# Clustered attention, a Fourier mix and a feed-forward layer on one core: scales of the weights from sums on TensorE, a later product with the values, and a cast moved to GpSimd

## The chip, the cores and the metric

The kernel runs on one core of a Trainium2 chip. A core has five engines that run on their own and wait for each other through semaphores: TensorE (PE, matrix products; its weight loads are shown apart as PEld), VectorE (DVE), ScalarE (ACT), GpSimd (POOL) and SyncE (SP, which here issues every DMA, in order). The metric is the device time of the whole program in microseconds (us), the median of the runs.

## The reference

Attention over 4 sequences of 768 tokens, 8 heads of 64; a query sees only the keys that are nearest to the same one of 16 centroids. Then a two-dimensional Fourier transform whose real part is added, a normalisation, and a feed-forward layer.

```python
mask = q_assign[:, :, :, None] == k_assign[:, :, None, :]
scores = np.where(mask, scale * np.matmul(q, k.transpose(0, 1, 3, 2)), -1e9)
attn = np.exp(scores - np.max(scores, axis=-1, keepdims=True))
attn = attn / (np.sum(attn, axis=-1, keepdims=True) + 1e-09)
x = np.matmul(attn, v)                       # heads side by side: (4, 768, 512)
u = x + np.real(np.fft.fft(np.fft.fft(x, axis=1), axis=2))
un = (u - mean(u)) / np.sqrt(var(u) + 1e-06)
out = u + np.maximum(un @ w_ch1, 0.0) @ w_ch2        # 512 x 2048 and 2048 x 512
```

The two weight matrices come as 64-bit floats. Products are made in 16-bit floats, with each operand split in a high and a low half.

## The kernel before, in words

`Overlap.run` lays the program out in ticks. Heads go in pairs: 4 pairs for a sequence, 16 in all. In each tick one strip of 128 queries of a pair gets its scores (`Attention.scores`), and the strip that stood `LAG` = 2 ticks earlier is multiplied with the values (`attend`). Six ticks make a pair, 24 a sequence. The next pair's preparation (`prep`: loading q and k, their scales, the split in halves, the cluster assignment, a one-hot table) is spread over the ticks before it. The order on TensorE is the order in which this code is written; on the other engines a scheduler sets it, with costs of its own, and the queues then run strictly in that order.

One strip of scores goes through all engines, twice, for the two heads of the pair (j = 0, 1). TensorE writes 128x768 scores in PSUM (L320, L325). VectorE scales them by a negative factor, writes the result (`ju`) and leaves the row's minimum in `m` (L339). ScalarE takes the exponential: in the first sequence ("early", `pr < 4`) from `ju`, which then lies in the not yet used second token buffer `X` (L343); in the later ones from the scores in PSUM (L345), and `ju` is then only a bfloat16 by-product. ScalarE casts the result to 16 bits, the high half (L353; `ph` for the first head, `p` for the second in the early ones). GpSimd subtracts to get the low half (L354). SyncE sends both through a transposing DMA to `pt` (L356), of which there are `PT` = 5, and TensorE multiplies `pt` with the values (L374 to L376) into `ps_o`, which VectorE empties after every third strip (L386 to L390).

The weights are made ready during the first sequence, by `Weights.run`, a step for each of 32 tiles of 128x512, 0.684 ticks apart. A tile's 512 KB land in one of 8 raw buffers. ScalarE turns the topmost 16 bits of each number in two patterns by sign (`signs`, L519 and L520), TensorE joins them (`join`, L528), VectorE puts in the lower bits (L532), and `halve` writes the scaled high and low halves. The scale is a power of two from the largest number: VectorE reduces every tile's top bits to its largest (`largest`, L491). For the first matrix four tiles share one scale over all partitions (L496, a broadcast `along` TensorE and L504); for the second each tile has its own for each partition, four at a time. `top_power` then makes the scale in four small instructions (L58 to L61), on 128x1 or 128x4 numbers. `relative` joins the scales of both matrices at the end.

From the second sequence on, the previous sequence's Fourier transform (`Fourier`) and feed-forward layer (`FeedForward`, L858 up and L888 down) are filled in between the ticks.

Of the kernel before, what the change touches and what calls it, by code (L numbers as in the profile page):

```python
# [16 lines left out]
I32 = mybir.dt.int32  # L17
# [36 lines left out]

def top_power(nc, tops, s, inv):

    t = tops.bitcast(I32)
    nc.vector.tensor_scalar(out=t, in0=t, scalar1=20, scalar2=None, op0=ALU.logical_shift_right)  # L58
    nc.vector.tensor_scalar(out=t, in0=t, scalar1=-910.0, scalar2=1.0, op0=ALU.add, op1=ALU.max)
    nc.vector.tensor_scalar(out=inv.bitcast(I32), in0=t, scalar1=240.0, scalar2=float(1 << 23), op0=ALU.min, op1=ALU.mult)  # L60
    nc.vector.reciprocal(out=s, in_=inv)  # L61
# [20 lines left out]
class Attention:  # L82
# [22 lines left out]
    EX = 1  # L105
    PC = ()

# [201 lines left out]
    def scores(self, pr, st):  # L309
        nc, sb = self.nc, self.sb  # L310
        assert self.ready >= pr
        (hq, hk), oh, (e, ne) = self.hl[pr], self.oht[pr], self.sc.scores(pr)
        sl = slice(st * P, (st + 1) * P)
# [13 lines left out]
        for j in range(2):  # L327

            m = sb.tile([P, 1], F32, name="rmx", tag="rmx", bufs=6)
            early = pr < H // 2  # L330
            if early:

                n = (2 * st + j) % self.RING * S
                p32 = self.X[1].rearrange("p a x -> p (a x)")[:, n:n + S]
            else:
                p32 = sb.tile([P, S], F32, name="p32", tag="p32", bufs=2)
            x = p32.rearrange("p (h x) -> p h x", h=2)
            ju = x if early else sb.tile([P, 2, SH], BF16, name="ju", tag="ju")
            self.mark = nc.vector.tensor_scalar(out=ju, in0=ps[j][:, :, 0:SH], scalar1=ne, scalar2=None, op0=ALU.mult, op1=ALU.min,  # L339
                                    accum_out=m)  # L340
            self.late = m
            if early:
                nc.scalar.activation(p32, p32, AF.Exp, bias=m, scale=-1.0)  # L343
            else:
                nc.scalar.activation(x, ps[j][:, :, 0:SH], AF.Exp, bias=m, scale=e)  # L345
            if early and j:
                ph = sb.tile([P, S], F32, name="p32", tag="p32", bufs=2).bitcast(F16).rearrange("p (a x) -> p a x", a=2)
            else:
                ph = sb.tile([P, 2, S], F16, name="ph", tag="ph", bufs=2)
            if early and j and (st in self.PC):  # L350
                nc.gpsimd.tensor_copy(out=ph[:, 0], in_=p32)
            else:
                nc.scalar.copy(out=ph[:, 0], in_=p32)  # L353
            nc.gpsimd.tensor_tensor(out=ph[:, 1], in0=p32, in1=ph[:, 0], op=ALU.subtract)  # L354
# [79 lines left out]
class Weights:  # L434
# [6 lines left out]

    RAW, PN = tuple(4128 * i for i in range(6)) + (29696, 33824), (24768, 26816)
    ID, TOP, MX = 28864, 29376, 29472
    X32 = 37952, 40000
    EXTRA, A2, AHEAD = 0, 9, 7

    def __init__(self, tc, pool, arena, psf, w1, w2, ident):
# [5 lines left out]

        self.inv = [pool.tile([P, n], F32, name=f"winv{n}") for n in (4, 16)]
        self.rel = pool.tile([P, 16], F32, name="wrel")
# [29 lines left out]

    def largest(self, k):

        nc, at = self.nc, self.arena.at
        g, i = divmod(k, 4)
        mx = at(self.MX + 32 * (g % 2), [P, 4], F32)  # L490
        nc.vector.tensor_reduce(out=mx[:, i:i + 1], in_=self.top(k).bitcast(BF16), op=ALU.max, axis=AX.X,  # L491
                                apply_absolute_value=True)
        if i == 3 and g >= 4:
            self.scales(g, mx)
        elif i == 3:
            nc.vector.tensor_reduce(out=mx[:, 0:1], in_=mx, op=ALU.max, axis=AX.X)  # L496

    def block(self, g):

        nc, at = self.nc, self.arena.at  # L500
        mx = at(self.MX + 32 * (g % 2), [P, 4], F32)
        ps = self.psf()
        along(nc, ps[:, 0:P], mx[:, 0:1], self.ident)
        nc.vector.tensor_reduce(out=mx[:, 1:2], in_=ps[:, 0:P], op=ALU.max, axis=AX.X)  # L504
        self.scales(g, mx[:, 1:2])

    def scales(self, g, mx):
        n = mx.shape[1]
        s = self.sb.tile([P, 4], F32, name="wsc", tag="wsc", bufs=2)
        top_power(self.nc, mx, s[:, 0:n], self.inv[0][:, g:g + 1] if n == 1 else self.inv[1][:, 4 * (g - 4):4 * (g - 3)])  # L510
        for i in range(4):
            self.scale[4 * g + i] = s[:, i % n:i % n + 1]

    def signs(self, k):

        nc, at = self.nc, self.arena.at
        pn = at(self.PN[k % 2], [P, 2, DM], BF16)
        top = self.top(k)
        nc.scalar.activation(pn[:, 0].bitcast(I16), top.bitcast(I16), AF.Relu, bias=self.off[:, 0:1], scale=8.0)  # L519
        nc.scalar.activation(pn[:, 1].bitcast(I16), top, AF.Relu, bias=self.off[:, 1:2], scale=8.0)  # L520
        self.bits[k] = pn

# [11 lines left out]
    def halve(self, k):  # L534
# [4 lines left out]
        if k % 2:  # L539
            x = self.arena.at(self.X32[k // 2 % 2], [P, DM], F32)  # L540
            nc.scalar.activation(x, ps, AF.Copy, scale=s)
# [4 lines left out]
    def run(self):  # L546
# [5 lines left out]
        for i in range(2):  # L552
            nc.gpsimd.tensor_scalar(out=self.idb[:, i], in0=self.ident, scalar1=1.0 - 2 * i, scalar2=None, op0=ALU.mult)
        for k in range(-self.AHEAD, 33):
            if k >= 1 and k % 4 == 1 and k < 16:
                self.block(k // 4)
# [14 lines left out]
    def relative(self):  # L571

        nc, at = self.nc, self.arena.at
        top, m1, r = (at(self.TOP + 32 * j, [P, 1], F32) for j in range(3))
        rel = self.rel
        nc.vector.tensor_tensor(out=rel.rearrange("p (a c) -> p a c", c=4),
                                in0=self.inv[1].rearrange("p (a c) -> p a c", c=4),
                                in1=self.inv[0].rearrange("p (a o) -> p a o", o=1).broadcast_to([P, 4, 4]), op=ALU.mult)
        nc.vector.tensor_reduce(out=m1, in_=rel, op=ALU.max, axis=AX.X)
        ps = self.psf()  # L580
        along(nc, ps[:, 0:P], m1, self.ident)
        nc.vector.tensor_reduce(out=top, in_=ps[:, 0:P], op=ALU.max, axis=AX.X)
        nc.vector.reciprocal(out=r, in_=top)
        nc.vector.tensor_scalar(out=rel, in0=rel, scalar1=r[:, 0:1], scalar2=HSC, op0=ALU.mult, op1=ALU.mult)
        nc.vector.tensor_scalar(out=self.dsc, in0=top, scalar1=1.0 / HSC, scalar2=None, op0=ALU.mult)

# [34 lines left out]
class Fourier:  # L621
# [25 lines left out]
    def fold(self, b):  # L647
# [4 lines left out]
        s = self.scale[b][0]  # L652
        mid = at(self.XM, [1, M + 1], F32)
        nc.gpsimd.tensor_copy(out=mid, in_=X[0:1, 3, 0:M + 1])
        nc.gpsimd.tensor_tensor(out=mid[:, 1:M], in0=mid[:, 1:M], in1=X[0:1, 3, DM - 1:M:-1], op=ALU.add)
        last = at(self.XL, [P, 3], F32)
        xt = {}
        for i, op in self.FOLDS:
# [8 lines left out]
            nc.sync.dma_start(out=t, in_=h.rearrange("p a t x -> p (a t x)"), transpose=True)  # L667
            xt[i] = t.rearrange("p (a t c) x -> p a t c x", a=2, t=3)
        self.parts[b] = xt, last, mid, s

# [117 lines left out]
USC = 200  # L788
HSC = float(2.0 ** -20)


class FeedForward:


    NT = 2 * P
    HH, HL, OSB, HR = 0, 8192, (16384, 18432), (28736, 29760)
# [48 lines left out]
    def up(self, blk):  # L845
# [6 lines left out]
        for f in range(16):  # L852
# [8 lines left out]
            r = at(self.HR[f % 2], [P, self.NT], F32)  # L861
            if f % 2:
                nc.vector.tensor_scalar(out=r, in0=ps, scalar1=rel[:, f:f + 1], scalar2=0.0, op0=ALU.mult, op1=ALU.max)  # L863
            else:
                nc.scalar.activation(r, ps, AF.Relu, scale=rel[:, f:f + 1])
            nc.scalar.activation(hh[:, f], ps, AF.Relu, scale=rel[:, f:f + 1])  # L866
            nc.gpsimd.tensor_tensor(out=hl[:, f], in0=r, in1=hh[:, f], op=ALU.subtract)  # L867
# [29 lines left out]

PT = 5


class Overlap:
# [22 lines left out]
    F2 = 1  # L924
    PIN, PF, PV = (), 29, 1
    CE, WP, WQ = 0.45, 0, 0

# [53 lines left out]
    def run(self):  # L981
# [43 lines left out]
        for pr in range(NP):  # L1025
# [36 lines left out]
def cluster_attention_fourier_ffn_kernel(ctx, tc, q, k, v, cent, w1, w2, cd, sd, cm, cs, ss, ny, out):  # L1062
# [5 lines left out]
    sc = Scales(nc, glob)  # L1068
    arena = Arena(glob, 47264)
    pf = ctx.enter_context(tc.tile_pool(name="ps_f", bufs=3, space=PSUM))  # L1070
# [46 lines left out]
```

## Time and profile before

| | |
|---|---|
| three runs | 1055.57, 1049.64, 1053.56 us; median 1053.56 |
| the profiled execution | 1049.91 us, its span 1048.1 us |
| busy in the span | PE 910.8 us (87%), DVE 627.4 (60%), ACT 625.3 (60%), POOL 586.9 (56%) |
| DMA queue of SP | 138.50 MB, 65.9% of 16 engines |
| first scores of pairs 0, 1, 2, 3 and 4 read by VectorE | at 31.1, 75.9, 125.6, 170.9 and 208.5 us |

How to read the page: the digits of its second part are tenths of a slice of 26.2 us in which an engine was busy; PEclk is the granted clock of TensorE; the DMA row is the mean busy share of the 16 DMA engines, and as a number it can go above 1, since packets overlap. A group's row tells its line, engine, operation, what it writes and reads, the count, busy time, the mean of one in ns, and the idle time of the engine before it with what ended that.

### The profile page before, as it was taken

The numbers are of one execution on the slowest core, as the hardware profiler recorded it, in microseconds if no ns is written. First come the engines' busy times: TensorE is split into PE (matmuls) and PEld (weight loads), VectorE is DVE, ScalarE is ACT, GpSimd is POOL, SyncE is SP. The second block draws the span as 40 slices with busy tenths as digits, with TensorE's granted clock in tenths as the row PEclk, the third lists the DMA queues.
The fourth block names the chain that finished last, engine by engine and source line by source line (L and its number), as shares of the span: only waits on it lengthen the run. The fifth ranks groups of instructions, "written<-read, shape, count | busy, mean of one in ns | idle before, by whom it ended". The sixth has DMA issues, their size and how long they took to land.

```text
span 1048.1 us, 23542 instructions
## 1 busy us (share of the span) xinstructions
PE 910.8 (87%) x9350; PEld 591.7 (56%) x9362; DVE 627.4 (60%) x1297; ACT 625.3 (60%) x980; POOL 586.9 (56%) x693
## 2 busy tenths in 40 slices
PE   3665565749899999998899999997999999999998
PEld 2333333425575756655666757555757667576674
DVE  8789899767757555668656555667555333631110
ACT  4798889755766665645666746556756543351230
POOL 2364565753975756655856646647847645271230
PEclk9987878769899999999899999998999999999999
DMA  7799998979887776568877767588757562321000
GB/s 272 179 225 245 196 239 166 171 156 153 177 123 153 128 154 121 121 137 161 153 137 142 140 128 132 110 141 170 124 102 133 96 110 43 81 52 31 11 11 21
DMA packets 396239, 140.01 MB, mean 134 GB/s; under 512 B 381784, under 2 KB 381792, under 8 KB 396128
## 3 DMA queue, kind: packets, MB, share of 16 engines
q1 hardware_dynamic: 396128, 138.50, 65.9%
q8 instruction: 73, 1.20, 0.5%
q14 instruction: 38, 0.31, 0.1%
HBM read 42.52 MB, written 6.29 MB: 47 GB/s over the span
## 4 chain that ended last, share of the span: by engine, by line
PE 39%; DVE 6%; DMA 3%; ACT 3%; POOL 2%; issue 2%; SPq 0%; ACTq 0%; DVEq 0%; POOLq 0%
PE ps_f L888 16%; PE ps_f L858 13%; PE ps_big L320 3%; DMA pt<-ph 3%; PE ps_f L713 2%; DVE ju L339 1%; ACT p L345 1%; PE ps_o L374 1%; POOL ph L354 1%; PE ps_o L375 1%; PE ps_o L376 1%; PE ps_big L325 1%; ACT ph L353 1%; DMA scr<-in_k_dram 0%; DVE arena L660 0%
## 5 line engine op out<-in xcount | busy, mean ns | idle before, releaser
L354 POOL TENSOR_TENSOR ph<-p,ph 128x768 f16<-128x768 f32 x144 | 242.9, 1688 | 184.6 <-ACT ph L353 150.1
L858 PE MATMUL ps_f<-arena,w1h 128*128 128x256 f16 x1536 | 271.4, 277 | 19.1 <-ACT arena L866 9.0
L888 PE MATMUL ps_f<-w2h,arena 128*128 128x512 f16 x768 | 238.9, 379 | 0.0
L345 ACT ACTIVATE p<-ps_big,rmx,sce 128x768 f32<-128x768 f32 x144 | 142.1, 988 | 132.9 <-DVE ju L339 127.5
L858 PE MATMUL ps_f<-arena,w1l 128*128 128x256 f16 x768 | 212.4, 277 | 0.0
L339 DVE TENSOR_SCALAR_CACHE_REDUCE ju<-ps_big,sce 128x768 bf16<-128x768 f32 x144 | 146.1, 1014 | 68.2 <-PE ps_big L325 58.2
L888 PEld LDWEIGHTS <-arena 128*128 128x128 f16 x1152 | 108.7, 98 | 126.6 <-issue 5.2
L858 PEld LDWEIGHTS <-w1h 128*128 128x128 f16 x1536 | 152.1, 99 | 36.0 <-issue 14.3
L867 POOL TENSOR_TENSOR arena<-arena 128x256 f16<-128x256 f32 x192 | 128.1, 677 | 77.3 <-ACT arena L866 73.6
L320 PE MATMUL ps_big<-hlk,hlq 64*128 64x384 f16 x1152 | 128.9, 348 | 39.0 <-ACT p L345 23.4
L374 PE MATMUL ps_o<-v,pt 128*128 128x66 f16 x1152 | 124.8, 198 | 43.0 <-DVE X L390 27.5
L888 PE MATMUL ps_f<-w2l,arena 128*128 128x512 f16 x384 | 145.5, 379 | 0.0
L374 PEld LDWEIGHTS <-pt 128*128 128x128 f16 x1152 | 110.2, 100 | 57.7 <-issue 37.1
L353 ACT CAST ph<-p 128x768 f16<-128x768 f32 x144 | 119.6, 832 | 15.0 <-DMA pt<-ph 12.8
L375 PE MATMUL ps_o<-v,pt 128*128 128x64 f16 x1152 | 124.8, 199 | 0.0
L376 PE MATMUL ps_o<-v,pt 128*128 128x66 f16 x1152 | 124.5, 198 | 0.0
L866 ACT ACTIVATE arena<-ps_f,wrel 128x256 f16<-128x256 f32 x192 | 90.1, 472 | 54.8 <-DVE arena L863 54.7
L863 DVE TENSOR_SCALAR arena<-ps_f,wrel 128x256 f32<-128x256 f32 x96 | 46.3, 482 | 124.9 <-PE ps_f L858 66.4
L320 PEld LDWEIGHTS <-hlq 64*128 64x128 f16 x1152 | 55.5, 99 | 101.5 <-issue 72.7
L375 PEld LDWEIGHTS <-pt 128*128 128x128 f16 x1152 | 110.7, 101 | 2.8
L376 PEld LDWEIGHTS <-pt 128*128 128x128 f16 x1152 | 111.1, 103 | 0.0
L858 PEld LDWEIGHTS <-w1l 128*128 128x128 f16 x768 | 76.1, 99 | 20.2 <-issue 10.7
(178 smaller groups left out, 1330.4 us busy)
## 6 DMA issues: line engine op xcount, KB each, us to landing
arena<-in_moe_w_ch_dram SPq DMA_DIRECT2D x32, 512.0 KB, 6.8
scr<-in_q_dram SPq DMA_DIRECT2D x16, 384.0 KB, 2.9
scr<-in_k_dram SPq DMA_DIRECT2D x16, 384.0 KB, 4.5
vst<-in_v_dram SPq DMA_DIRECT2D x16, 384.0 KB, 3.5
out_dram<-arena SPq DMA_DIRECT2D x24, 256.0 KB, 2.3
pt<-ph SPq DMA_TRANSPOSE x168, 3.9
arena<-in_cs_dram SPq DMA_DIRECT2D x12, 192.0 KB, 3.5
arena<-in_ss_dram SPq DMA_DIRECT2D x12, 192.0 KB, 3.5
```

Of the source, the lines that this page charges most:

```text
L320: nc.tensor.matmul(out=ps[j][:, hf, 0:SH], lhsT=hq[rows[j], a, sl], rhs=hk[rows[j], c, hs], start=(i == 0), stop=False)
L339: self.mark = nc.vector.tensor_scalar(out=ju, in0=ps[j][:, :, 0:SH], scalar1=ne, scalar2=None, op0=ALU.mult, op1=ALU.min, accum_out=m)
L345: nc.scalar.activation(x, ps[j][:, :, 0:SH], AF.Exp, bias=m, scale=e)
L353: nc.scalar.copy(out=ph[:, 0], in_=p32)
L354: nc.gpsimd.tensor_tensor(out=ph[:, 1], in0=p32, in1=ph[:, 0], op=ALU.subtract)
L374: nc.tensor.matmul(out=o[:, at:at + W], lhsT=hi, rhs=v16[:, kt, 0:W], start=(kt == 0), stop=False)
L375: nc.tensor.matmul(out=o[:, at:at + D], lhsT=hi, rhs=v16[:, kt, 66:130], start=False, stop=False)
L376: nc.tensor.matmul(out=o[:, at:at + W], lhsT=lo, rhs=v16[:, kt, 0:W], start=False, stop=(kt == ST - 1))
L858: nc.tensor.matmul(out=ps.rearrange("p (t x) -> p t x", x=P), lhsT=a[:, dc, fs], rhs=c[:, :, dc], start=(i == 0), stop=(i == 11))
L866: nc.scalar.activation(hh[:, f], ps, AF.Relu, scale=rel[:, f:f + 1])
L867: nc.gpsimd.tensor_tensor(out=hl[:, f], in0=r, in1=hh[:, f], op=ALU.subtract)
L888: nc.tensor.matmul(out=ps, lhsT=a[:, f, ts], rhs=c[:, f], start=(i == 0), stop=(i == 47))
```

## The change

The largest number of a tile is no longer searched. The two sign patterns of four tiles (a group) are summed over the partitions by eight products with a matrix of ones (`block`, L490), all in one PSUM tile; the largest entry of that sum, its exponent taken, gives one scale for the group, in both matrices. `signs` handles two tiles in one instruction, with three buffers for the patterns. `top_power` writes to PSUM and works on 128x1 in all eight groups. In the first sequence the high half of the second head is cast by GpSimd (L347). In later sequences `ju` is written in place in PSUM as a float, and ScalarE reads it from there. The product with the values comes three ticks behind the scores in the first 22 strips, with six `pt`. `relative` is shorter, and GpSimd's two small instructions for `mid` come after the folds.

```diff
-    PC = ()
...
-            ju = x if early else sb.tile([P, 2, SH], BF16, name="ju", tag="ju")
+            ju = x if early else ps[j][:, :, 0:SH]
...
-            if early:
-                nc.scalar.activation(p32, p32, AF.Exp, bias=m, scale=-1.0)
-            else:
-                nc.scalar.activation(x, ps[j][:, :, 0:SH], AF.Exp, bias=m, scale=e)
+            nc.scalar.activation(x, ju, AF.Exp, bias=m, scale=-1.0)
...
-            if early and j and (st in self.PC):
+            if early and j:
                 nc.gpsimd.tensor_copy(out=ph[:, 0], in_=p32)
...
-    def largest(self, k):
...
-        nc.vector.tensor_reduce(out=mx[:, i:i + 1], in_=self.top(k).bitcast(BF16), op=ALU.max, axis=AX.X,
-                                apply_absolute_value=True)
...
+        ps = self.psf()
+        i = 0
+        for k in range(4 * g, 4 * g + 4):
+            for j in range(2):
+                nc.tensor.matmul(out=ps, lhsT=self.ones[:, 0:1].broadcast_to([P, P]), rhs=self.bits[k][:, j], start=(i == 0), stop=(i == 7))
+                i += 1
+        mx = at(self.MX + 32 * (g % 2), [P, 1], F32)
+        nc.vector.tensor_reduce(out=mx, in_=ps, op=ALU.max, axis=AX.X)
+        s = self.sb.tile([P, 1], F32, name="wsc", tag="wsc", bufs=2)
+        top_power(nc, mx, ps[:, 0:1], s, self.inv[g // 4][:, g % 4:g % 4 + 1])
...
-            if 0 <= k + 3 < 32:
-                self.largest(k + 3)
-            if 0 <= k + 1 < 32:
-                self.signs(k + 1)
+            if k % 2 == 0 and 0 <= k + 2 < 32:
+                self.signs(k + 2)
+            if k % 4 == 0 and 0 <= k < 32:
+                self.block(k // 4)
...
-PT = 5
+PT = 6
...
-                at(t0 + st + self.LAG, 3, att.attend, pr, st)
+                at(t0 + st + self.LAG + (6 * pr + st < self.LATE), 3, att.attend, pr, st)
```

What the queues make of it is shown at three places. The first is VectorE's queue where the second matrix gets its first group's scale, in the third pair of heads; `arena` holds the raw weights, `X_64` the early `ju`. Before:

```order
L491 TENSOR_REDUCE arena<-arena 128x1
L544 SCALAR_TENSOR_TENSOR w2l<-ps_f,wsc,w2h 128x512
L58 TENSOR_SCALAR arena<-arena 128x4
L59 TENSOR_SCALAR arena<-arena 128x4
L60 TENSOR_SCALAR winv_86<-arena 128x4
L61 RECIPROCAL wsc<-winv_86 128x4
L491 TENSOR_REDUCE arena<-arena 128x1
L532 SCALAR_TENSOR_TENSOR ps_f<-arena,ps_f 128x512
```

After:

```order
L493 TENSOR_REDUCE arena<-ps_f 128x1
L518 SCALAR_TENSOR_TENSOR ps_f<-arena,ps_f 128x512
L58 TENSOR_SCALAR ps_f<-arena 128x1
L215 TENSOR_REDUCE amx<-scr 128x1
L59 TENSOR_SCALAR ps_f<-ps_f 128x1
L60 TENSOR_SCALAR winv_86<-ps_f 128x1
L61 RECIPROCAL wsc<-winv_86 128x1
```

The reductions L491 of single tiles are gone; one reduction of a group's sum (L493) stands ahead of the four small instructions, which are now one number wide.

The second is TensorE's queue ahead of the first scores (L320 before), where the first pair's transposes (L271 before, L270 after) end. Before:

```order
L271 MATMUL ps_f<-ident,ac 128x128 x3
L528 LDWEIGHTS arena
L528 MATMUL ps_f<-arena 128x512
L528 LDWEIGHTS arena
L528 MATMUL ps_f<-arena 128x512
L48 MATMUL ps_f<-ident,amx 128x128 x3
```

After, the end of the eight products of the first group's sum, of which the last three are shown, and the join (now L514):

```order
L490 LDWEIGHTS arena
L490 MATMUL ps_f<-arena 128x512
L490 LDWEIGHTS arena
L490 MATMUL ps_f<-arena 128x512
L490 LDWEIGHTS arena
L490 MATMUL ps_f<-arena 128x512
L514 LDWEIGHTS arena
L514 MATMUL ps_f<-arena 128x512
L514 LDWEIGHTS arena
L514 MATMUL ps_f<-arena 128x512
```

Such a run of eight products comes eight times, each time with a tick's scores queued behind it.

The third is GpSimd's queue at the first strips of the first pair. Before:

```order
L354 TENSOR_TENSOR ph<-X_64,ph 128x768
L354 TENSOR_TENSOR p_299<-X_64,p_299 128x768
L542 TENSOR_TENSOR w1l<-arena,w1h 128x512
L189 COPY vst<-rmx 128x1
L354 TENSOR_TENSOR ph<-X_64,ph 128x768
```

After:

```order
L347 CAST p_310<-X_64 128x768
L350 TENSOR_TENSOR ph<-X_64,ph 128x768
L528 TENSOR_TENSOR w1l<-arena,w1h 128x512
L350 TENSOR_TENSOR p_310<-X_64,p_310 128x768
L188 COPY vst<-rmx 128x1
L347 CAST p_357<-X_64 128x768
```

The second head's cast stands ahead of the first head's subtraction.

More of the change, by code (lines that the diff above doesn't have):

```diff
@@ L434 @@
 class Weights:
[L442 to L444 removed]
+    RAW, PN = tuple(4128 * i for i in range(6)) + (29696, 33824), (24768, 40000, 44096)
+    ID, TOP, MX, ONE = 28864, 29376, 29472, 29568
+    X32 = 37952
     EXTRA, A2, AHEAD = 0, 9, 7
@@ L452, in __init__ @@
         self.dsc = pool.tile([P, 1], F32, name="dsc")
-        self.inv = [pool.tile([P, n], F32, name=f"winv{n}") for n in (4, 16)]
+        self.inv = [pool.tile([P, 4], F32, name=f"winv{n}") for n in range(2)]
         self.rel = pool.tile([P, 16], F32, name="wrel")
```

81 lines of the change are left out of this document (33 added, 48 removed).

## The prediction

> **What bounds the kernel now.** I read the busy time by stage first, to see where time can come from at all. Columns: window, its length, busy time and count of each engine, granted TensorE clock, DMA share, GB/s.
>
> ```profile
> core 0: us, PE busy (x) PEld busy (x) DVE busy (x) ACT busy (x) POOL busy (x), PEclk, DMA share, GB/s
> 0.00:31.00 31.00, 12.95 (x52) 6.60 (x53) 25.04 (x72) 15.15 (x24) 5.54 (x38) 1.00 0.68 239
> 31.00:208.00 177.00, 110.58 (x1313) 65.58 (x1324) 151.08 (x311) 153.17 (x219) 105.02 (x90) 0.83 0.96 207
> 208.00:1048.00 840.00, 787.26 (x7987) 519.56 (x7985) 451.27 (x915) 456.95 (x739) 476.32 (x566) 0.97 0.60 114
> ```
>
> The three windows are the start, the first sequence's strips and the rest. In the rest TensorE is busy 787.3 of 840 us (94%), and none of its products there is touched. In the middle 177 us it works only 62%, while DVE (85%) and ACT (87%) are nearly full, and so are the DMA engines. By pair of heads:
>
> ```profile
> 31.00:76.00 45.00, 29.00 (x314) 15.74 (x318) 35.65 (x84) 39.76 (x58) 25.95 (x20) 0.92 0.98 215
> 76.00:125.60 49.60, 28.00 (x358) 17.25 (x358) 44.55 (x89) 43.09 (x63) 28.48 (x26) 0.83 0.95 228
> 125.60:171.00 45.40, 29.23 (x348) 17.60 (x351) 41.98 (x82) 40.71 (x59) 26.36 (x22) 0.77 0.99 209
> 171.00:208.00 37.00, 24.35 (x300) 14.99 (x300) 28.91 (x61) 29.61 (x42) 24.22 (x22) 0.77 0.88 164
> ```
>
> The fourth pair, with no L491 left and few weights, takes 37 us; the three others take 45 to 50. Then TensorE's waits from 25 to 210 us (engine, tile, line, by whom, us in total, times, longest):
>
> ```profile
> PE ps_o L374 <- DVE X L390: 27.5, 6, 5.5
> PE ps_big L320 <- DVE X L339: 14.8, 17, 3.7
> PE ps_o L374 <- DMA pt<-p: 8.6, 8, 2.6
> PE ps_o L374 <- DMA pt<-ph: 6.8, 4, 2.2
> ```
>
> It waits mostly for DVE. Last, one such wait from inside: DVE's timeline before the first scores of the third pair (start, length).
>
> ```profile
> 116.50 1.61 DVE L59 TENSOR_SCALAR arena<-arena 128x4 int32<-128x4 int32 x1
> 118.15 1.56 DVE L60 TENSOR_SCALAR winv<-arena 128x4 int32<-128x4 int32 x1
> ...
> 123.38 1.71 DVE L236 SCALAR_TENSOR_TENSOR hlq<-scr,scp,hlq 128x768 f16<-128x768 f32 x1 [0.52 <-ACT hlq L235]
> 125.01 0.67 DVE L491 TENSOR_REDUCE arena<-arena 128x1 f32<-128x512 bf16 x1
> 125.60 1.00 DVE L339 TENSOR_SCALAR_CACHE_REDUCE X<-ps_big,sce 128x768 f32<-128x768 f32 x1
> ```
>
> and POOL's at the same time:
>
> ```profile
> 116.44 1.64 POOL L354 TENSOR_TENSOR ph<-X,ph 128x768 f16<-128x768 f32 x1 [0.41 <-DVE w2l L544]
> 118.05 1.64 POOL L354 TENSOR_TENSOR p<-X,p 128x768 f16<-128x768 f32 x1
> ...
> 123.12 1.15 POOL L542 TENSOR_TENSOR w2l<-arena,w2h 128x512 f16<-128x512 f32 x1
> ```
>
> Two instructions on four numbers last 1.6 us each, and each ends within 0.03 us of a POOL subtraction's end (118.11 and 118.08; 119.71 and 119.69): they sit out POOL's instruction. So the stage is DVE's and ACT's, in strict order, with DMA close behind.
>
> **The change part by part.** The rows of the groups (whole run or the first 210 us, which for these are the same):
>
> ```profile
> L491 DVE TENSOR_REDUCE arena<-arena 128x1 f32<-128x512 bf16 x32 | 21.7, 680 | 8.0 <-DMA arena<-in_moe_w_ch_dram 7.9
> L504 DVE TENSOR_REDUCE arena<-ps_f 128x1 f32<-128x128 f32 x4 | 1.1, 284 | 0.6 <-PE ps_f L48 0.6
> L59 DVE TENSOR_SCALAR arena<-arena 128x4 int32<-128x4 int32 x4 | 4.6, 1143 | 0.1
> L60 DVE TENSOR_SCALAR winv<-arena 128x4 int32<-128x4 int32 x4 | 6.2, 1547 | 0.1
> L59 DVE TENSOR_SCALAR arena<-arena 128x1 int32<-128x1 int32 x4 | 0.6, 148 | 0.0
> L60 DVE TENSOR_SCALAR winv<-arena 128x1 int32<-128x1 int32 x4 | 0.6, 151 | 0.1
> L519 ACT ACTIVATE arena<-arena 128x512 int16<-128x512 int16 x32 | 24.1, 753 | 4.6 <-PE ps_f L528 1.6 <-PE ps_o L376 1.5 <-DMA scr<-in_q_dram 1.5
> L343 ACT ACTIVATE X<-X,rmx 128x768 f32<-128x768 f32 x48 | 44.1, 935 | 9.3 <-DVE X L339 7.6 <-POOL ph L354 1.4 <-issue 0.3
> L353 ACT CAST p<-X 128x768 f16<-128x768 f32 x24 | 20.0, 833 | 0.0
> L528 PE MATMUL ps_f<-arena 128*128 128x512 bf16 x52 | 22.0, 510 | 6.8 <-DVE w1l L544 4.6 <-DVE arena L58 1.0 <-issue 0.7
> ```
>
> DVE. Gone: 21.7 (L491), 1.1 (L504), 10.8 (the 4-wide L59 and L60). Added: eight reductions of 512 sums, 0.68 each as L491 (5.4), and four more groups of 1-wide L59 and L60 (4 x 0.30 = 1.2). L58 and L61 stay at eight each. Net 33.6 - 6.6 = 27 us less. Eight of the L491 lie before 31 us (columns as in the first windows, of L491 alone):
>
> ```profile
> 0.00:31.00 31.00, 5.41 (x8) 1.00 0.68 239
> ```
>
> so the stage loses about 22 us of DVE's 151.
>
> ACT. 24 casts go: 20.0. The 64 sign patterns of 512 become 32 of 1024. L519 and L343, both with a pointer as bias, give (935 - 753)/256 = 0.71 ns an element, so 1.12 us: 32 x 1.12 = 36 against 64 x 0.75 = 48, 12 less (ends: 0, if 1024 costs twice 512, and 15). Together 32, of which some 29 in the stage.
>
> POOL gets the 24 casts. No such cast is in the trace; the nearest copies are these, the upper end is L354, with two inputs, at 1.64:
>
> ```profile
> L882 POOL COPY arena<-X 128x512 f32<-128x512 f32 x4 | 2.5, 612 | 0.0
> L654 POOL COPY arena<-X 1x257 f32<-1x257 f32 x4 | 1.6, 391 | 0.1
> ```
>
> 221 ns for 255 elements more, so 0.83 us for 768, which I take as nearest in kind: 20 us (ends 15 and 39). POOL goes from 105 to 125 of the stage. The cast takes as long as ACT's 0.83 and runs beside ACT's cast of the first head, so both `pt` are issued no later.
>
> TensorE gets 64 products like L528: 22.0/52 = 0.42 us each, 27 us, eight at a time, 3.4 us ahead of a tick's scores. Its sign patterns are queued on ACT before the exponentials of the ticks ahead, so I see no wait for ACT there. TensorE goes from 111 to some 135: it stays below DVE and has 66 us of waits in the stage to lose.
>
> The third tick of distance gives the `pt` transposes 7 us more to land; that removes the 15.4 us of waits for `pt` above, and part of the 27.5 for `ps_o`, which is DVE's lateness; I count both as how the relief comes through, not again. With six `pt`, a transpose now waits for the product three strips back, which is queued right behind this tick's scores, while the transpose needs DVE, ACT and POOL first (L339 1.00, L343 0.94, L353 0.83 and L354 1.64, 4.4 us): no wait.
>
> `ju` in PSUM (144 times, after 208 us): a DVE write to PSUM costs 688 ns (L532) where one to SBUF costs 737 (L544), both with 512 elements:
>
> ```profile
> L532 DVE SCALAR_TENSOR_TENSOR ps_f<-arena,ps_f 128x512 uint32<-128x512 uint32 x32 | 21.5, 688 | 3.3 <-PE ps_f L528 3.2
> L544 DVE SCALAR_TENSOR_TENSOR w2l<-ps_f,wsc,w2h 128x512 f16<-128x512 f32 x8 | 5.9, 737 | 0.0
> PE ps_big L320 <- ACT p L345: 10.1, 8, 3.0
> ```
>
> ACT already waited for DVE's minimum, so the chain is the same; TensorE's products hide it. The last row is what TensorE waits there for `ps_big` after 260 us. I take 0, ends -4 and +4. The later `mid` and the shorter `relative` are 1 us each off the path: 0.
>
> DMA moves the same bytes, and is next. Its best over 25 us is here:
>
> ```profile
> 50.00:75.00 25.00, 15.48 (x193) 9.36 (x192) 20.11 (x52) 23.70 (x35) 17.02 (x13) 0.86 1.07 224
> 75.00:100.00 25.00, 14.67 (x216) 9.41 (x218) 23.18 (x46) 21.83 (x33) 12.26 (x11) 0.80 1.07 252
> ```
>
> **The sum.** The stage holds 0.96 x 177 = 170 us of DMA work; at 1.07 that needs 159 us, 18 less than now. By DVE, 129 us at its 85% make 151 us, 26 less. DMA ends first: I take 16 of its 18. In the start the eight L491 (5.4 us, on a DVE busy 81%) stand partly between the first pair's steps: 3 less (ends 0 and 5). Total -19: 1049.9 - 19 = 1031 against the profiled execution, whose span is 1048.1. That execution lies 3.7 below the median of the runs shown (1053.56); a new kernel's median may lie off its best as well, so 1032.
>
> A page would give more: by "DMA: Bandwidth & Descriptors" of the Trainium skill, section "Latency and other measured facts", a transposing DMA reaches 261 GB/s; moving the stage's 207 GB/s x 177 us at that rate is, as an estimate, 140 us, so DMA would not bind and the sum would be -29, 1021. The trace never held more than 252 GB/s there, with the share at 1.07, so I keep the bound.
>
> **The rivals.**
> (a) DMA holds the stage as it is: its share is 0.95 to 0.99 over three pairs already, and overlapping packets may be no reserve. Against it: 1.07 over 50 us, and DMA waits of 15 us beside 42 for DVE. Only the start and 2 us come: 1045 to 1050.
> (b) All of DVE's relief comes through: 26 + 5: 1018 to 1022. For it: the fourth pair's 37 us; against: DMA.
> (c) Slower: TensorE's sums come before the scores in a queue in strict order. If their 27 us lie open, they eat the relief of 19: +8, 1058. That decides from 70% of them uncovered. Against it: the 66 us TensorE idles there.
> (d) POOL's casts hold DVE. L236 at 123.38 lasted 1.71, where 768 elements take L339 1.00, beside POOL's instruction of 123.12. If each of 24 casts did that for its 0.83 us, 20 us would go: 1050. "SBUF — State Buffer" of the Trainium skill, "Who interferes with whom", has the rule: VectorE in a two-port mode, or with two SBUF inputs, and GpSimd share a port pair under an exclusive lock. The two fences of 116 to 120 us agree. But only L236, L201 and the one-hot steps, some 7 a pair, are of that kind, and the 4-wide ones leave.
>
> **How the numbers follow.** Forecast (1024 to 1041) 0.60; (b) 0.14; (a) 0.13; (d) 0.06; (c) 0.07. The range reaches from (b)'s 1018 into (a), 1047. A change below 0.5% (5.3 us) can't be told from none. Faster, below 1048.3: 0.60 + 0.14 + 0.10 of (a) = 0.84; same: the rest of (a) and (d) 0.09; slower 0.07.
>
> **What would show it.** Right: first scores of the fifth pair at DVE near 189 instead of 208.5 us; DVE busy near 600; DMA share above 1.0 from 50 to 170 us; the casts on POOL near 0.83 us; the later stretch as long as before. Wrong: a stage near 177 us with the DMA share unchanged (a); TensorE waiting at the sums, or scores late behind them (c); longer L235 and L200 rows (d); POOL over 90% in the stage, if the cast costs as much as a subtraction.

## The result, and the profile after

Slower, where the prediction said faster: 1060.57 us median (1058.07 to 1062.89, 6 runs) against 1051.39 for the kernel before on the same chip (1049.64 to 1055.57, 6 runs). The ratio is 1.0081, with a 95% interval of 1.0059 to 1.0103. The forecast was 1032, its range 1018 to 1047.

The windows of the changed kernel, cut at the same places as before (first scores of the first and the fifth pair; same columns):

```profile
29.80:215.00 185.20, 121.50 (x1324) 69.43 (x1343) 136.05 (x287) 130.28 (x165) 123.02 (x114) 0.77 0.90 199
215.00:1057.80 842.80, 790.58 (x8017) 521.87 (x8016) 449.98 (x913) 441.81 (x737) 477.66 (x566) 0.97 0.59 114
```

The first sequence takes 185.2 us instead of 177, the rest 842.8 instead of 840. VectorE's work there fell from 151 to 136 us and ACT's from 153 to 130 (some 129 and 124 were forecast), and both are used less: VectorE 73% of the stage (it was 85%), ACT 70% (87%), GpSimd 66%, DMA 0.90 (0.96). No engine is near full. TensorE's granted clock is 0.77 there (it was 0.83). By pair:

```profile
29.80:73.50 43.70, 29.15 (x274) 14.82 (x278) 34.68 (x73) 37.16 (x47) 28.17 (x25) 0.77 0.90 221
73.50:122.10 48.60, 33.47 (x380) 19.49 (x386) 34.07 (x76) 34.18 (x43) 33.30 (x33) 0.78 0.97 221
122.10:168.50 46.40, 30.22 (x326) 18.00 (x331) 33.09 (x73) 33.96 (x43) 28.95 (x27) 0.76 0.95 200
168.50:215.00 46.50, 28.66 (x351) 17.11 (x352) 34.21 (x69) 24.98 (x33) 32.60 (x31) 0.76 0.78 156
```

The fourth pair lost most: 46.5 us instead of 37, with ACT busy 54%. Now the sizes of what was added, by groups of the whole run:

```profile
L347 POOL CAST p<-X 128x768 f16<-128x768 f32 x24 | 19.9, 828 | 36.9 <-ACT X L341 25.4 <-DMA pt<-p 9.3 <-ACT ph L349 1.3
L505 ACT ACTIVATE arena<-arena 128x1024 int16<-128x1024 int16 x16 | 19.5, 1218 | 3.3 <-PE ps_f L514 2.2 <-DMA arena<-in_moe_w_ch_dram 0.9 <-PE ps_o L372 0.2
L490 PE MATMUL ps_f<-arena 128*128 128x512 bf16 x60 | 18.3, 444 | 3.8 <-DVE w1l L530 3.2 <-issue 0.4
L493 DVE TENSOR_REDUCE arena<-ps_f 128x1 f32<-128x512 f32 x8 | 5.4, 680 | 0.0
```

The prices were right: the cast costs 0.828 us (0.83 was taken), a product of the sums 0.444 (0.42), the reduction 0.680 (0.68). What is new is the idle time in front of the cast, 36.9 us: GpSimd stands there with the cast at the head of its queue, for the exponential and for the buffer `p`. And the waits of TensorE and VectorE from 25 to 215 us (us, times, longest):

```profile
PE ps_big L319 <- DVE X L338: 34.5, 18, 7.9
PE ps_o L370 <- DVE X L386: 7.4, 1, 7.4
...
PE ps_o L370 <- DMA pt<-p: 0.5, 2, 0.3
...
DVE amx L247 <- DMA vst<-in_v_dram: 10.9, 2, 7.3
DVE amx L215 <- DMA scr<-in_q_dram: 9.6, 4, 4.8
DVE X L338 <- PE ps_big L324: 6.6, 7, 2.6
DVE w1l L530 <- ACT w1h L524: 5.9, 3, 3.2
```

The waits for `pt` are gone, as the third tick was to do, and the wait for `ps_o` to be emptied fell from 27.5 to 7.4 us. In their place TensorE waits 34.5 us (14.8 before) for VectorE to read scores, and VectorE, which should have been the fuller one, waits itself: 20.5 us for loads of v and q (5.0 before). One such wait, on VectorE, then the wait of SyncE's queue (SPq) that went ahead of it (the longest of its two, 5.2 us), and the queue itself:

```profile
138.35 0.08 DVE L338 DVE_READ_ACCUMULATOR X<-ps_big,sce 128x1 f32 x1
145.73 0.95 DVE L247 TENSOR_REDUCE amx<-vst 128x1 f32<-128x768 f32 x1 [7.29 <-DMA vst<-in_v_dram]
```

```profile
SPq L480 <- DVE ps_f L58: 5.7, 2, 5.2
```

```profile
132.57 0.33 SPq L480 DMA_DIRECT2D arena<-in_moe_w_ch_dram  x1
133.00 1.27 SPq L352 DMA_TRANSPOSE pt<-p  x1
134.37 3.44 SPq L352 DMA_TRANSPOSE pt<-ph  x1
137.91 1.46 SPq L352 DMA_TRANSPOSE pt<-p  x1
139.47 1.78 SPq L352 DMA_TRANSPOSE pt<-ph  x1
141.35 1.16 SPq L189 DMA_DIRECT2D vst<-in_v_dram  x1
```

GpSimd's small copy that lets this load go (L188) ran at 134.91. The load was issued at 141.35, since three transposes stood ahead of it in SyncE's queue. These did not wait for GpSimd any more: their subtractions had ended 5 to 7 us before they were issued (at 127.49, 132.54 and 134.22). The queue itself was late. It had stood from 127.31 to 132.57 with the load of a weight tile at its head, for VectorE to be done with the buffer (L518, which ended at 132.54), and then took 1.3 to 3.4 us for each transpose. VectorE, in strict order as well, did nothing for 7.29 us, and the score reads queued behind the reduction waited too. So here VectorE held SyncE's queue first and that queue VectorE afterwards.

### The profile page after: what moved, and what is told of

Its sections match the earlier page's. It is cut to its first block, busy times and chain, and to the rows that moved or that the text cites. A ratio compares the mean times of both kernels' runs of the same rounds, so it can differ in the third digit from the quotient of the medians.

```text
span 1057.8 us, 23533 instructions
## 1 busy us (share of the span) xinstructions
PE 926.0 (88%) x9396; PEld 598.0 (57%) x9416; DVE 606.7 (57%) x1264; ACT 589.3 (56%) x924; POOL 606.2 (57%) x718
## 4 chain that ended last, share of the span: by engine, by line
PE 50%; DVE 14%; DMA 11%; POOL 8%; issue 8%; ACT 7%; SPq 1%; ACTq 0%; DVEq 0%; POOLq 0%
PE ps_f L872 20%; PE ps_f L841 16%; PE ps_big L319 5%; DMA vst<-in_v_dram 4%; DMA pt<-ph 4%; DVE ps_big L338 3%; POOL ph L350 3%; DMA pt<-p 2%; ACT ph L349 2%; PE ps_o L370 2%; PE ps_o L372 1%; PE ps_o L371 1%; PE ps_big L324 1%; DVE X L338 1%; PE ps_f L696 1%
## 5 line engine op out<-in xcount | busy, mean ns | idle before, releaser
L341 ACT ACTIVATE p<-ps_big,rmx 128x768 f32<-128x768 f32 x144 | 128.7, 899 | 128.6 <-DVE ps_big L338 115.5
L319 PE MATMUL ps_big<-hlk,hlq 64*128 64x384 f16 x1152 | 131.4, 351 | 54.1 <-DVE X L338 34.5
L338 DVE TENSOR_SCALAR_CACHE_REDUCE ps_big<-ps_big,sce 128x768 f32<-128x768 f32 x144 | 141.5, 1020 | 47.9 <-PE ps_big L324 47.8
L349 ACT CAST ph<-p 128x768 f16<-128x768 f32 x144 | 118.1, 832 | 20.7 <-DMA pt<-ph 19.9
```

What stands on the lines that cost most here:

```text
L319: nc.tensor.matmul(out=ps[j][:, hf, 0:SH], lhsT=hq[rows[j], a, sl], rhs=hk[rows[j], c, hs], start=(i == 0), stop=False)
L341: nc.scalar.activation(x, ju, AF.Exp, bias=m, scale=-1.0)
```

## The experiments

The theories have letters in the expectations. C: the casts on GpSimd cost the time. L: the third tick. W: TensorE's sums. J: `ju` in PSUM. Q: the scheduler, which sees other costs, has put VectorE's reductions of loads ahead of its score reads. Times are medians, ratios are to the kernel before on the same chip.

**One part undone at a time.** With the casts of the second heads back on ACT:

```diff
-            if early and j:
+            if early and j and False:
                 nc.gpsimd.tensor_copy(out=ph[:, 0], in_=p32)
```

> The changed kernel with the second heads' cast back on ScalarE. Theory C (GpSimd's casts lengthen the chain, since GpSimd waited 25.4 us for ACT's exponentials and 9.3 us for the pt transposes at L347): about 10 us less than the changed kernel, near the kernel before. Theory Q (VectorE's queue is what costs: reductions of q, k and v stand ahead of the score reads and wait 20 us for their loads): the order changes with it, but the waits for loads stay; within 4 us of the changed kernel.

1044.48 us (1043.01 to 1045.66), ratio 0.9915 [0.9884, 0.9946]: the one undone line gives 16 us and makes the change a gain. Its stage, and TensorE's wait for score reads from 25 to 215 us:

```profile
30.40:192.00 161.60, 113.80 (x1337) 64.27 (x1356) 134.47 (x285) 143.19 (x187) 103.28 (x89) 0.84 1.02 224
192.00:1043.80 851.80, 794.69 (x8008) 521.57 (x8004) 450.80 (x916) 444.58 (x740) 480.38 (x567) 0.97 0.59 113
```

```profile
PE ps_big L319 <- DVE X L338: 12.8, 14, 2.9
```

161.6 us instead of 185.2, with the same VectorE work (134.5 and 136.1 us) and 13 us more on ACT. Of the 23.6 us, 9 are given back later (851.8 against 842.8). VectorE's waits for loads in the same window:

```profile
DVE amx L215 <- DMA scr<-in_q_dram: 11.2, 5, 4.8
...
DVE amx L247 <- DMA vst<-in_v_dram: 4.8, 4, 2.1
```

They are still 16.0 us, of 20.5, so late loads alone don't make the difference. Two other things in the traces do differ. The first is SyncE's queue. It issues the transposes in the order of the strips, in both kernels. With the casts on ACT, GpSimd makes the subtractions in that order too; with the casts on GpSimd it swaps five times a strip's second head with the first head of the next strip, and a transpose that is ready stands behind one that isn't. One first head's, ready at 168.01 us, was issued at 176.49, behind that of the second head before it, which was ready at 170.38 and issued at 173.68. From the end of a subtraction to the issue of its transpose the mean is 2.5 us (first heads) and 2.0 us (second heads) in the changed kernel, and 0.6 and 0.8 us here. The second is TensorE's granted clock, 0.84 here and 0.77 there: the same products keep TensorE busy for 113.8 and for 121.5 us. Whether the lower clock lengthens the stage or comes of it, no run separates.

With two ticks and five `pt` again (`LATE = 0`, `PT = 5`):

> The changed kernel with a distance of two ticks throughout and five pt. Theory L (with three ticks a pt transpose waits for a product further back, and SyncE's queue with the loads behind it): about 10 us less than the changed kernel. Theory Q: within 4 us of it, or some us more, as TensorE's 15 us of waits for pt come back.

1067.47, ratio 1.0137 [1.0110, 1.0164]. With the weights' part of the kernel before (L491, 4-wide scales, patterns of one tile):

> The changed kernel with the weights' scales as before (reductions of single tiles on VectorE, no sums on TensorE). Theory W (the sums stand open in TensorE's queue): about 10 us less than the changed kernel. Theory Q: VectorE has 27 us more to do and fewer waits for loads; within 5 us of the changed kernel, since its freed time went into waits.

1065.98, ratio 1.0128 [1.0095, 1.0161]. So both parts help the changed kernel. With `ju` as before and two ticks (`ju` alone has no room in memory beside six `pt`):

> The changed kernel with ju as before (bfloat16 in SBUF, the exponential from the scores) and a distance of two ticks with five pt, for which alone there is room. Theory J (ju in PSUM holds the later stretch, 3 us longer in the changed kernel): 3 us less than the same kernel with the distance alone undone. Otherwise equal to it within 2 us.

1064.57, ratio 1.0109 [1.0082, 1.0137]: 2.9 us below the run with two ticks alone, which is what `ju` in PSUM costs there.

**One part alone.** The weights' part in the kernel before (casts on ACT, two ticks, `ju` as before):

> The kernel before with the weights' part of the change alone (sums by TensorE, sign patterns of 1024, top_power on PSUM); casts on ACT, two ticks, ju in SBUF as before. W (the relief of DVE is real and was eaten by the casts): faster than before, 1036 to 1044, since the weights of before cost the changed kernel 5.4 us more and the run with the casts on ACT was 7 below before. L (the third tick is needed for it): 1048 to 1055. Rival (the weights' part is worth nothing without the emptier ACT): 1050.

1057.46, ratio 1.0050 [1.0027, 1.0073]: neither gain nor nothing, a loss of 5 us. What TensorE waits there from 25 to 210 us:

```profile
PE ps_o L373 <- DMA pt<-p: 27.1, 13, 6.8
...
PE ps_o L373 <- DMA pt<-ph: 9.2, 7, 3.8
```

36.3 us for `pt`, where the kernel before waits 15.4. The third tick and `ju` without the weights' part:

> The kernel before with the third tick and ju in PSUM alone: weights' scales as before, casts on ACT. If the third tick's gain stands by itself: 1042 to 1048. If it only pays for TensorE's sums (which the kernel with the weights' part alone had ahead of its scores): 1049 to 1054, so that weights and tick are a gain together only.

1056.31, ratio 1.0032 [1.0015, 1.0050]. Alone each of the two costs 4 to 6 us; together (the run with the casts on ACT) they save 7. The cast alone, in the kernel before (`PC = (0, 1, 2, 3, 4, 5)`):

> The kernel before with the cast of the second heads on GpSimd and nothing else. C: slower than before by 8 to 20 us, 1060 to 1072. Q (order by accident): anything within 5 us of before, to be read against VectorE's order. My recorded step (the cast costs no time and frees 20 us of ACT): 1045 to 1052.

1062.84, ratio 1.0097 [1.0059, 1.0135]. TensorE's waits for `pt` there, from 25 to 219 us:

```profile
PE ps_o L374 <- DMA pt<-p: 25.9, 12, 5.4
...
PE ps_o L374 <- DMA pt<-ph: 10.5, 4, 6.6
```

36.4 us instead of 15.4. From the start of a strip's score read to the end of its subtraction, the mean over the 24 strips went from 8.19 to 8.85 us for the second head (first head 7.41 and 7.16): the scheduler put the cast ahead of the first head's subtraction, and the second head's then stands behind both. Up to the issue of the transpose it went from 8.7 to 9.8 us for the second head and from 7.8 to 8.1 for the first, so both `pt` are issued later.

Put beside each other, the same cast in five settings (not all pairs on one chip; the kernel before takes 1051.4 to 1052.8 us on all of them):

| else in the kernel | cast on ACT | cast on GpSimd | difference |
|---|---|---|---|
| as before | 1051 to 1053 | 1062.84 | about 11 |
| weights' part | 1057.46 | 1064.57 | 7 |
| third tick, `ju` | 1056.31 | 1065.98 | 10 |
| all of the change | 1044.48 | 1060.57 | 16 |
| all, VectorE's order pinned (below) | 1045.22 | 1059.69 | 14 |

**The order of VectorE's queue.** The preparation's steps and the splits of v are put behind the tick's last score read, so that the order of score reads, reductions and splits is regular:

```diff
-    PIN, PF, PV = (), 29, 1
+    PIN, PF, PV = (1, 2, 4), 0, 1
```

> The changed kernel with steps 1, 2 and 4 of the preparation and the splits of v issued behind the tick's last read of scores, so that VectorE's reductions of loads never stand ahead of score reads (the order is regular in all sequences). Q (the harm is VectorE's order, shuffled by the cast): 1040 to 1048, stage near 165 us. C (the cast itself, as work of GpSimd in the chain and beside VectorE): 1056 to 1065, stage 180 us or more.

> The same pinned kernel with the cast of the second heads back on ACT; the order of score reads, reductions and splits on VectorE is the same as in the pinned kernel with the cast on GpSimd. Q: within 4 us of that kernel, both near 1044. C: 12 to 20 us below that kernel.

1059.69, ratio 1.0071 [1.0046, 1.0095], with the cast on GpSimd; 1045.22, ratio 0.9932 [0.9908, 0.9956], with it on ACT. Q falls: with the same order of those instructions in both, the cast costs 14 us, and pinning itself moves either kernel by 1 us. The two stages, GpSimd's first, and the splits of v in them:

```profile
30.40:208.30 177.90, 114.35 (x1324) 64.60 (x1345) 141.56 (x285) 130.72 (x166) 124.98 (x114) 0.82 0.92 206
...
L200 DVE SCALAR_TENSOR_TENSOR v<-vst,scp,v 128x384 f16<-128x384 f32 x8 | 10.8, 1355 | 0.2 <-ACT v L198 0.2
```

```profile
30.00:198.90 168.90, 111.18 (x1325) 60.75 (x1344) 133.88 (x286) 146.11 (x190) 104.80 (x90) 0.84 1.03 219
...
L200 DVE SCALAR_TENSOR_TENSOR v<-vst,scp,v 128x384 f16<-128x384 f32 x8 | 7.1, 892 | 0.0
```

VectorE no longer waits for loads here, but the same instructions take it 7.7 us longer beside GpSimd's casts, 3.7 of them in L200, where the stage is 9.0 us longer. That the one makes the other is likely and not shown; in the unpinned pair VectorE's work differed by only 1.6 us (136.05 and 134.47). TensorE's busy time differs by 3.2 us here (clock 0.82 and 0.84), by 7.7 in the unpinned pair. The cost has no fixed place.

**Is it the cast's place, or GpSimd's load?** The kernel with the casts on ACT gets one more copy on GpSimd for each second head. Nobody reads its result, and in the trace no engine waits for it:

```diff
             nc.gpsimd.tensor_tensor(out=ph[:, 1], in0=p32, in1=ph[:, 0], op=ALU.subtract)
+            if early and j:
+                nc.gpsimd.tensor_copy(out=p32, in_=p32)
```

> The changed kernel with the cast of the second heads on ACT, and one more copy on GpSimd for each second head of the first sequence (768 float32 onto themselves, behind the subtraction): GpSimd's work as in the changed kernel or more, and no cast in the chain from exponential to transpose. G (GpSimd's load: its time, or what it holds up at VectorE and in its own queue): most of the loss comes back, 1055 to 1062. K (the cast's place in the chain, ahead of the first head's subtraction and waiting for the exponential at the head of GpSimd's queue): within 4 us of the kernel with the casts on ACT, 1044 to 1048.

1058.72 (1053.09 to 1061.43), ratio 1.0059 [1.0037, 1.0082]. And the changed kernel with the cast queued behind the first head's subtraction (`with self.tc.issue_after(sub.ins)` around it):

> The changed kernel with GpSimd's cast of a second head queued behind the subtraction of the same strip's first head. K (what costs is the cast at the head of the queue, waiting for the exponential): 1045 to 1051. G (GpSimd's load): 1056 to 1064 as the changed kernel.

1064.23, ratio 1.0116 [1.0084, 1.0149]. K falls by both: 20 us of idle copies bring 14 of the 16 us, and another place in the queue brings nothing. The first of the two (its profiled execution, of 1053.09 us, is the shortest of its ten, so less of the loss shows in it):

```profile
28.60:202.10 173.50, 120.00 (x1326) 66.41 (x1345) 134.06 (x286) 147.07 (x189) 122.63 (x113) 0.79 0.99 212
...
L352 POOL COPY X<-X 128x768 f32<-128x768 f32 x24 | 20.4, 851 | 0.4
```

VectorE has the same work as with no copies (134.06 and 134.47 us) in a stage 12 us longer: here it is waits, not drawn-out rows, and TensorE waits 31.5 us for score reads where it waited 12.8. GpSimd is busy 71%. The transposes are issued as soon after their subtractions as with no copies (0.5 and 0.8 us), so the swapped order of the changed kernel is not needed for the loss; the clock is low here too (0.79, TensorE busy 120.0 us).

**Any engine's load?** The same copy, but on ACT (`nc.scalar.copy(out=p32, in_=p32)`):

> The kernel with all casts on ACT, and one more copy of 768 elements on ACT for each second head, behind the cast: the idle work of GpSimd's run put on ACT instead, some 19 us, so that ACT stands above 95% of its shorter stage. If 20 us on any of the engines in this loop cost so much: 1056 to 1064. If it is GpSimd's work alone that is dear: 1044 to 1050.

1057.62, ratio 1.0050 [1.0031, 1.0069]: 13 us for 20.0 us of copies.

```profile
30.10:208.30 178.20, 120.19 (x1325) 66.31 (x1344) 131.19 (x286) 160.14 (x210) 105.25 (x90) 0.78 0.95 203
...
L352 ACT COPY X<-X 128x768 f32<-128x768 f32 x24 | 20.0, 835 | 5.0 <-POOL p L350 5.0
```

```profile
DVE X L338 <- ACT X L352: 3.3, 4, 1.0
```

ACT was not filled up by them (90% of the longer stage, where 95% of a shorter one was expected): the stage grew by 17 us instead. So added work isn't dear on GpSimd alone. The copy on ACT is no idle work only, though: it has to wait for GpSimd's subtraction, which reads the same buffer (5.0 us), and VectorE waits for it (3.3 us). How much of the 13 us is the work alone is therefore open; on GpSimd, where nothing waits for the copy, 14 of 20.4 us come out as time.

**By which way?** In the changed kernel the loads of v for the second to sixth pair, and those of q and k for the third to sixth, go to ACT's DMA queue, away from the transposes in SyncE's:

```diff
-        nc.sync.dma_start(out=t, in_=self.v[b, :, 2 * hp:2 * hp + 2])
+        (nc.scalar if 0 < pr < 6 else nc.sync).dma_start(out=t, in_=self.v[b, :, 2 * hp:2 * hp + 2])
...
-            self.nc.sync.dma_start(out=t[:, side], in_=(self.q, self.k)[side][b, hp])
+            (self.nc.scalar if 1 < pr < 6 else self.nc.sync).dma_start(out=t[:, side], in_=(self.q, self.k)[side][b, hp])
```

> The changed kernel with the loads of q, k and v for the second to sixth pair issued by ACT's queue, so that they no longer stand behind the pt transposes (which wait for GpSimd's subtractions) in SyncE's. R (GpSimd's longer work reaches VectorE by way of SyncE's queue, as loads that come late): VectorE's waits for loads fall from 20 us to below 8, and the time to 1046 to 1053. D (the delay is spread over all the queues that meet in the loop, and the loads are one sign of it): 1056 to 1064.

1051.72, ratio 1.0006 [0.9986, 1.0025]: 9 of the 16 us are back. The stage, and VectorE's waits for loads from 25 to 215 us:

```profile
28.90:204.70 175.80, 119.53 (x1325) 66.61 (x1345) 137.46 (x288) 130.18 (x166) 125.42 (x114) 0.79 0.97 210
```

```profile
DVE amx L215 <- DMA scr<-in_q_dram: 10.1, 5, 4.1
...
DVE amx L247 <- DMA vst<-in_v_dram: 4.1, 3, 2.4
...
DVE amx L215 <- DMA scr<-in_k_dram: 3.4, 2, 2.0
```

The 7.3 us wait for v is gone, but the waits for loads are still 17.6 us, of 20.5, where less than 8 was expected. So the time is as R says and its sign is missing. The thirteen loads that were moved took 9.0 us of SyncE's queue in the changed kernel. Whether the time comes back because they arrive earlier, or because that queue is free for the transposes, no run separates.

**Does DMA hold the stage?** The kernel with the casts on ACT, loading half the columns of weight tiles 8 to 31:

> The kernel with the casts on ACT, with only half the columns of weight tiles 8 to 31 loaded (the other half keeps what stands in the buffer, so the weights are not the reference's). If DMA holds its first sequence (its share is 1.12 over two pairs, where my prediction's bound was 1.07): 1034 to 1040, the stage 10 us shorter. If DMA is only busy: 1043 to 1046.

1040.60 (1038.96 to 1045.96), ratio 0.9896 [0.9857, 0.9935]: between the two expectations. The profiled executions of this kernel and of the one it is compared with are each the longest of their four (1045.96 and 1045.66 us), and the stage is no shorter:

```profile
29.60:193.10 163.50, 117.23 (x1325) 65.24 (x1344) 133.79 (x286) 144.03 (x188) 104.43 (x90) 0.80 0.93 185
```

163.5 us at a DMA share of 0.93, against 161.6 at 1.02. So DMA alone does not set the length. The medians differ by 3.9 us (1044.48 and 1040.60), with intervals that overlap, so that DMA holds a few us is not excluded.

**A better kernel.** The casts on ACT, `ju` in SBUF as before, three ticks with five `pt`:

> The kernel with all casts on ACT, with ju in SBUF as before and five pt in place of six. ju in SBUF gave 3 us with two ticks; if that holds and five pt do for three ticks: 1040 to 1043, the best kernel. If five pt are too few for three ticks: slower, 1046 to 1060, with TensorE or ACT waiting for pt.

1039.62 (1036.63 to 1040.41), ratio 0.9874 [0.9848, 0.9900]: the best kernel, 1.3% faster than before.

```profile
27.80:190.80 163.00, 109.62 (x1337) 62.60 (x1357) 136.41 (x285) 143.20 (x187) 103.06 (x89) 0.87 1.02 222
190.80:1037.30 846.50, 793.25 (x8007) 521.92 (x8003) 454.51 (x916) 457.83 (x740) 478.25 (x567) 0.97 0.59 114
```

Five `pt` are enough for three ticks. Against the run with the weights' part alone (1057.46) only the third tick is added: it is worth 18 us there. With its loads on ACT's queue as well:

> The best kernel so far (casts on ACT, ju in SBUF, three ticks, five pt) with the loads of the second to sixth pair issued by ACT's queue. With the casts back, VectorE waits only 8.5 us for loads there, and ACT is the busiest engine. If late loads still cost: 1033 to 1038. If the waits that ACT's queue now takes (a load stands at its head until its buffer is free) cost as much: 1038 to 1046.

1039.27, ratio 0.9863 [0.9825, 0.9901]: the same. The detour of the loads paid in the changed kernel and does not here.

## Why the prediction was wrong, point by point

- **The failed step** is the one on GpSimd: "The cast takes as long as ACT's 0.83 and runs beside ACT's cast of the first head, so both `pt` are issued no later", with nothing for it in the sum. The price was right (0.828 us), the overlap was not: the cast cost 7 to 16 us in five settings, 16 in the changed kernel. In the kernel before with the cast alone, the second heads' `pt` are issued 1.1 us later and the first heads' 0.3 us, and TensorE's waits for `pt` rise by 21 us. In the changed kernel the third tick covers these waits, and in their place TensorE waits 34.5 us for score reads, where 12.8 remain without the casts. Moving the loads to another queue brings 9 of the 16 us back. The way from the cast to the end stays open.
- **How much of the miss that is**: the forecast lay 28.6 us too low, and 16 of them are the cast. Without it the stage is as short as forecast (161.6 us, where 177 less 16 was taken), and the other 12 are mostly the later stretch (below).
- **Behind it, the way of summing.** I took each engine's busy time, set it against its best share so far (DVE 85%, DMA 1.07), and let the fullest resource give the length. The stage is a loop of queues in strict order, and added work costs in it though no engine is full: 14 us for 20 of idle copies on an engine 71% busy. GpSimd's idle 72 of 177 us, which I took for room, was time in which GpSimd waited for others, and the others waited for it in turn.
- **VectorE's and ACT's relief**: right in size, for the terms named. DVE fell from 627.4 to 606.7 us, 20.7 where 27 was forecast: the rows named fell by 27, and some 7 us went to others (`ju` in PSUM, below, is one). ACT fell from 625.3 to 589.3, 36 where 32 was taken: the casts 20.0, the patterns 9.3 (12 taken), and, not foreseen, the later exponentials 13.4. These are sums of rows, which overlap, so they come to more than the 36.
- **The DMA floor** of 159 us: a stage of 161.6 us came once the casts were back, but not by this cause alone. With half the columns of 24 weight tiles not loaded the stage was as long in the profiled execution, and the time 3.9 us lower. The share, too, went above my 1.07:

```profile
73.30:113.20 39.90, 29.35 (x379) 17.83 (x383) 35.78 (x75) 38.35 (x51) 27.82 (x24) 0.87 1.12 240
```

  This is the second pair of the kernel with the casts on ACT. Rival (a), by which the stage could hardly get shorter, falls by the 161.6 us. The estimate from "DMA: Bandwidth & Descriptors" of the Trainium skill went by 261 GB/s; a pair of that kernel moved 244 at most, below it, and no run shows either as the limit.
- **The third tick**: its mechanism was right (15.4 us of waits for `pt` are 0.5), and it is worth more than I counted. Two ticks cost the changed kernel 7 us; with the casts on ACT and `ju` as before the third tick takes 1057.46 to 1039.62.
- **TensorE's sums, rival (c)**: with 1058 it names the time nearly, but not the cause. Undoing the weights' part made the changed kernel slower by 5.4 us. With two ticks that part alone does cost 5 us, but TensorE waits there for `pt`, not at the sums. That the scores queued behind the sums make `pt` late in that kernel was not tried.
- **Port lock, rival (d)**: the wrong account for this kernel. L200 and L235 were taken to show it, and VectorE's busy time in the stage differs by 1.6 us with and without the casts. In the pinned order it was 7.7. "SBUF — State Buffer" of the Trainium skill, "Who interferes with whom", has the exclusive lock between VectorE and GpSimd; L200's 1355 ns with the cast on GpSimd and 892 without agree with it. How much it costs depends on what happens to meet.
- **`ju` in PSUM**: taken as 0 with ends of -4 and +4; 2.9 us of cost measured with two ticks, and 4.9 between 1044.48 and 1039.62 (where one `pt` fewer comes with it). The write costs what I said (1020 ns, 1015 before), and ACT gained 13 us on the exponential. What I left out is the readout of the row's minimum behind the write; the last two rows are those after and before:

```profile
L338 DVE TENSOR_SCALAR_CACHE_REDUCE ps_big<-ps_big,sce 128x768 f32<-128x768 f32 x144 | 141.5, 1020 | 47.9 <-PE ps_big L324 47.8
L341 ACT ACTIVATE p<-ps_big,rmx 128x768 f32<-128x768 f32 x144 | 128.7, 899 | 128.6 <-DVE ps_big L338 115.5 <-POOL ph L350 5.5 <-POOL rpow L824 3.3
L338 DVE DVE_READ_ACCUMULATOR ps_big<-ps_big,sce 128x1 f32 x144 | 20.3, 141 | 0.0
L339 DVE DVE_READ_ACCUMULATOR ju<-ps_big,sce 128x1 f32 x144 | 11.9, 83 | 0.0
```

  The exponential was 988 ns with the scores read directly. The readout takes 58 ns more. That this is what the variant costs is not shown.
- **The later stretch as long as before**: 842.8 and 839.5 us, as forecast within 3.3. In the kernel with the casts on ACT, 851.8: part of a shorter stage is given back, which no step of mine held. Of the 12 us more than before, 3 lie in the fifth and sixth pair, 5 between them and the last 237 us (499.0 against 494.1; the changed kernel has 499.8 there too), and 4 in those last 237 us, at a clock of 0.98 where the changed kernel has 231.7 us at 1.00. Why was not tried.

Left open: by which waits the cast's cost reaches the end. Late transposes, late loads, drawn-out rows of VectorE and a lower clock of TensorE each go with it in some of the pairs, and no run isolates one. That the cast on GpSimd is what costs is shown; the way is not.

## What to carry to other kernels

Where several engines hand a strip round in queues of strict order, idle time isn't room: before counting moved work as hidden, look at what the idle engine waits for, and at whether the move changes the order in which it serves the next queue. Here the move cost a third to four fifths of its own 20 us. An idle copy put into the loop measures that, if no engine has to wait for the copy. Parts of a change can each lose alone and win together (weights' part +5, third tick and `ju` +4, both -7), and one of them can hide the gain of all the rest, so undo them one at a time.

## What the runs showed of the hardware that was not expected

- Issuing loads from another engine's queue can be worth time: 9 us in the changed kernel (1060.57 and 1051.72), nothing in the best one (1039.62 and 1039.27). "Trainium Kernel Development and Optimization" of the Trainium skill, "Key Constraints", says that issuing from several engines saves only the sequencer's issue time. The loads moved took 9.0 us of SyncE's queue in the changed kernel and 6.4 in the best one, so no run here shows more than that.
- A transpose that was ready at 127.49 us was issued at 134.37: SyncE's queue stood 5.1 us of that with the load of a weight tile at its head, which waited for its buffer.
- The readout of VectorE's accumulated minimum took 141 ns where the numbers went to PSUM and 83 where they went to SBUF.
- 20.4 us of copies on GpSimd that no engine waited for cost 14 us. 20.0 us of copies on ACT cost 13, with waits for and by the copy of 8.3 us in them.
